# Joint attention block with 64-wide values tiles and re-placed transfers, and new orders in turned rows, route, second layer and last products of an attention-MoE kernel

## The chip, the cores and the metric

The kernel runs on one core of a Trainium2 chip. The metric is device time of one execution in microseconds; several runs are summed up by their median. The engines are TensorE (PE, with its weight loads as PEld), VectorE (DVE), ScalarE (ACT), GpSimd (POOL) and SyncE (SP), which issues most of the DMAs.

## The reference

Three parts follow one another: attention with a bias that a small MLP makes from positions, a top-1 mixture of experts with a capacity, and a two-matrix layer with h·cos(h).

```python
scores = scale * np.matmul(q, k.transpose(0, 1, 3, 2))        # B 2, H 8, S 576, D 64
h = np.maximum((psi_rel / psi_i)[..., None] @ w1 + b1, 0.0)   # log1p tables, hidden 32
scores = scores + (h @ w2).transpose(2, 0, 1)[None]
attn = np.exp(scores - np.max(scores, axis=-1, keepdims=True))
attn = attn / (np.sum(attn, axis=-1, keepdims=True) + 1e-09)
x = np.matmul(attn, v)                                        # to 1152 rows of 512
...
expert_idx = np.argmax(x @ w_gate, axis=1)                    # 8 experts
# the first 288 rows of each expert, in order, are kept
h = np.maximum(np.einsum('ecd,edf->ecf', disp, w1), 0.0)
y = np.einsum('ecf,efd->ecd', h, w2)
out[i] = gate_w[i] * y[expert_idx[i], pos[i]]                 # kept rows only
...
h = x @ w_in                                                  # 512 -> 2048
g = h * np.cos(h)
return g @ w_out
```

## The kernel before, in words

**Attention** (some 24 to 176 us) goes through 36 steps. A step is a batch, a block of 128 query rows and a pair of heads p; a block is four steps. `BLOCKS` orders them: (batch, block) (0,0), (1,0), (0,1), (1,1), then the **joint block** (block 4, which has only 64 rows, of both batches at once; steps 16 to 19), then (0,2), (1,2), (0,3), (1,3). `step_of(n)` writes a step out by hand: q·k products of step n+1 (`emit_qk`), the sum of scores and bias with the row minimum on DVE (`emit_sum`), the exponential on ACT (`emit_exp`), the transposes of step n (`emit_tr`) and their copies to SBUF on ACT (`emit_tev`), the values products of step n-1 (`emit_pv`) and their eviction (`emit_xs`), and the bias of group n+10 (`bias_h`, `bias_half`). At a step's end SP issues that step's transfers. Each engine runs its instructions in the order in which they are written here; `manual_schedule` reorders nothing. With the trace, the start of a step is the first q·k product (L403) that it issues.

**Bias.** 40 groups of rows: h = relu of a table row on DVE or ACT (L319 is on ACT, L321 on DVE; four quads to a group), a product (L347), the eviction with a scale into a row buffer `ev` (L351, L353), and a transfer from there to its place (L328, for the joint block L338). From group 14 on three `ev` buffers are used in rotation. The joint block's bias lands for one batch's 64 partitions; `double(p)` (L835) copies it on SP for the other batch, two heads at a time, in four steps from `DOUBLE_AT`. `fill_rows` (L840) and `fill_out` (L843) write zeros to the dispatch rows and to the output, at `FILL_AT` and `OUT_AT`. `emit_pv` makes the values products in column tiles of 32, four of them side by side; in the joint block separately for each batch, over 64 streamed columns instead of 128.

**Mixture of experts.** `route()` takes logits, the expert, the gate (L586 to L593) and the place of each row through running counts `srun`. The two fullest experts and a small one are done in straight line, others under a branch that isn't taken here. The fullest is chosen early, the second choice (L684 to L677) at `SECOND_CHOICE`. Expert 0's rows are gathered, turned by PE (`turned`, L990) and split into high and low parts (`xh` L991, `xl` L992), because a 32-bit product is made of three products of such parts. Its first products (L1018) start in the last attention steps. `e0_mid` and `e0_side` are tables of what goes between them; `f1` in them is the logits product of the last block (L544).

**Second layer** (some 246 to 352 us) has 16 slices f of 128 hidden columns. `first(f)` gives h on PE (L1281), in two parts of columns; `gate(f)` makes g of it: turns (copies on ACT, L1388, L1389), turn (L1392, DVE), sine (L1395, ACT), product (L1399, DVE), high (gh, L1402, ACT), low_ (gl, L1405, DVE). `second(f)` adds the slice's products into five tiles of 128 rows of output (L1377). The weights w_in and w_out are 64-bit numbers; `narrow` makes 32-bit ones of a piece by bit operations: mag (ACT, L754), then shift, low and sign (DVE, L757, L760, L763). `splitwi` and `splitwo` split them (high parts L962 on ACT, low parts L964 on DVE). `between(f)` sets the order of gate, narrowing and splits. At the end ACT and DVE evict the five tiles (L1362, L1364) and POOL stores them by indirect DMA (L1365).

## Time and profile before

| what | value |
|---|---|
| median of 3 runs | 361.13 us (360.67 to 361.41) |
| profiled execution | 361.79 us, its span 360.0 us |
[...]
| PE busy | 341.8 us, 95% of the span |
| DVE busy | 293.9 us, 82% |
| ACT busy | 266.8 us, 74% |
| POOL busy | 37.7 us, 10% |
| instruction queues | 37 packets (0.61 MB) and 24 packets (0.20 MB) |

The time is 1.8 us longer than the span, which goes from the first to the last instruction. An engine's busy share is an average over phases with different limits. In the timeline a line gives the start, the busy time, the engine, the line of the kernel, the operation, its output and input, the number of like operations in a row, and in brackets the idle time before it with what ended it. Matmul records overlap: the distance of two starts is what one costs, not its busy time.

### The profile page before, as it was taken

The numbers are of one execution on the slowest core, as the hardware profiler recorded it, in microseconds if no ns is written. First come the engines' busy times: TensorE is split into PE (matmuls) and PEld (weight loads), VectorE is DVE, ScalarE is ACT, GpSimd is POOL, SyncE is SP. The second block draws the span as 40 slices with busy tenths as digits, with TensorE's granted clock in tenths as the row PEclk, the third lists the DMA queues.
The fourth block names the chain that finished last, engine by engine and source line by source line (L and its number), as shares of the span: only waits on it lengthen the run. The fifth ranks groups of instructions, "written<-read, shape, count | busy, mean of one in ns | idle before, by whom it ended". The sixth has DMA issues, their size and how long they took to land. (4 is left out here: it accounts for less than half of the span.)

```text
span 360.0 us, 11244 instructions
## 1 busy us (share of the span) xinstructions
PE 341.8 (95%) x4459; PEld 272.8 (76%) x4459; DVE 293.9 (82%) x771; ACT 266.8 (74%) x627; POOL 37.7 (10%) x89
## 2 busy tenths in 40 slices
PE   7989999999989999898999999999999999999991
PEld 6346777775656777686789999968898898898880
DVE  5988889898869886988799999887997887876760
ACT  6768999987978898898943597387777667666560
POOL 3000001101001420110007112100000000000023
PEclk9999999999999999999999999999999999999997
DMA  7799966679976687799238698943243242110003
GB/s 234 203 246 278 251 168 194 203 157 258 277 244 190 205 247 192 249 258 310 90 109 309 167 353 280 295 157 119 66 121 107 91 131 73 58 62 0 2 28 117
DMA packets 47023, 63.89 MB, mean 177 GB/s; under 512 B 5772, under 2 KB 30476, under 8 KB 46962
## 3 DMA queue, kind: packets, MB, share of 16 engines
q1 hardware_dynamic: 45666, 60.24, 57.8%
q0 software_dynamic: 1152, 2.48, 1.9%
q8 instruction: 37, 0.61, 0.7%
q10 hardware_dynamic: 144, 0.36, 0.3%
q14 instruction: 24, 0.20, 0.2%
HBM read 41.08 MB, written 11.47 MB: 146 GB/s over the span
## 5 line engine op out<-in xcount | busy, mean ns | idle before, releaser
L420 ACT ACTIVATE e<-e,mn 128x576 f32<-128x576 f32 x72 | 56.2, 781 | 14.8 <-DVE mn L411 14.8
L321 DVE TENSOR_SCALAR h<-tt,sml 128x576 f32<-128x576 f32 x122 | 57.0, 513 | 0.1
L451 ACT ACTIVATE et<-t 128x512 f32<-128x512 f32 x72 | 38.7, 593 | 0.0
L347 PE MATMUL bb<-h,sml 128*32 128x288 f32 x400 | 35.6, 412 | 1.1 <-DVE h L321 0.6
L428 PEld LDWEIGHTS t<-ident,e 64*128 64x128 f32 x576 | 24.3, 139 | 8.9 <-issue 1.8
L403 PE MATMUL sb<-k,q 64*128 64x288 f32 (+1 forms) x160 | 27.0, 449 | 0.4 <-DVE lp L556 0.3
L353 ACT ACTIVATE wo<-bb,sml 128x288 f32<-128x288 f32 x49 | 24.7, 504 | 3.5 <-PE bb L347 2.1
L428 PE MATMUL t<-ident,e 64*128 64x64 f32 x576 | 26.1, 225 | 1.1 <-ACT e L420 0.8
L1281 PE MATMUL t<-yh,s1h 128*128 128x352 f32 (+1 forms) x88 | 26.8, 305 | 0.0
L1281 PE MATMUL t<-yh,s1l 128*128 128x352 f32 (+1 forms) x88 | 26.6, 303 | 0.0
L1281 PE MATMUL t<-yl,s1h 128*128 128x352 f32 (+1 forms) x88 | 26.5, 302 | 0.0
L1392 DVE TENSOR_TENSOR tn<-tn,kn 128x608 f32<-128x608 f32 (+2 forms) x18 | 13.0, 722 | 15.8 <-ACT kn L1389 15.7
L470 PE MATMUL sa<-et,wi 128*32 128x128 f32 (+1 forms) x800 | 23.0, 260 | 1.6 <-issue 1.6
L1402 ACT ACTIVATE gh<-tn 128x608 fp32r<-128x608 f32 (+2 forms) x18 | 11.8, 656 | 17.0 <-DVE tn L1399 17.0
L403 PE MATMUL sa<-k,q 64*128 64x288 f32 (+1 forms) x160 | 23.8, 406 | 0.0
L470 PEld LDWEIGHTS sa<-et,wi 128*32 128x32 f32 x800 | 19.5, 110 | 3.9 <-issue 1.7
L403 PEld LDWEIGHTS sb<-k,q 64*128 64x128 f32 (+1 forms) x160 | 10.5, 174 | 14.7 <-issue 6.0
L1018 PE MATMUL hp<-xh,s1h 128*128 128x288 f32 x64 | 19.5, 305 | 0.0
L1377 PE MATMUL hp<-s2h,gh 128*128 128x512 f32 x48 | 19.1, 399 | 0.0
L1021 ACT ACTIVATE hh<-hp 128x288 fp32r<-128x288 f32 x16 | 6.5, 409 | 17.0 <-PE hp L1018 17.0
L1377 PE MATMUL hp<-s2l,gh 128*128 128x512 f32 x48 | 19.0, 396 | 0.0
L1377 PE MATMUL hp<-s2h,gl 128*128 128x512 f32 x48 | 18.9, 394 | 0.0
(308 smaller groups left out, 999.9 us busy)
## 6 DMA issues: line engine op xcount, KB each, us to landing
keep<-win SPq DMA_DIRECT2D x16, 512.0 KB
keep<-wout SPq DMA_DIRECT2D x16, 512.0 KB
w1r<-mw SPq DMA_DIRECT2D x12, 512.0 KB
w2r<-mw SPq DMA_DIRECT2D x12, 512.0 KB
disp<-wo SPq DMA_DIRECT2D x10, 516.0 KB
bias<-wo SPq DMA_DIRECT2D x15, 288.0 KB
q<-qd SPq DMA_DIRECT2D x8, 512.0 KB
k<-kd SPq DMA_DIRECT2D x8, 288.0 KB
```

What stands on the lines that cost most here:

```text
L321: V.tensor_scalar(out=h, in0=win_, scalar1=col, scalar2=0.0, op0=ALU.add, op1=ALU.max)
L347: T.matmul(out=ps[32 * j:32 * j + 32, :], lhsT=w2s, rhs=h_t[g, j][:, cols], start=True, stop=True)
L353: A.activation(out=ev_t[g][:, cols], in_=ps, func=AF.Copy, scale=rst[:, g:g + 1])
L403: T.matmul(out=ps[a:e, half, 0:HS], lhsT=qt[b, ib][rows_, h, a:e], rhs=kt[c, p][rows_, u, :], start=True, stop=True)
L420: A.activation(out=e_t[n][:, u], in_=e_t[n][:, u], func=AF.Exp, scale=-1.0, bias=mn_t[n][:, u:u + 1], accum_out=z_t[b, ib][:, h:h + 1],)
L428: T.transpose(ps, src[half], ident[half, half])
L451: A.activation(out=et_t[n][:, 0:8, 64 * g:64 * g + 64], in_=halves[g], func=AF.Copy)
L470: T.matmul(out=xo[32 * i:32 * i + 32], lhsT=v_of(c, p, at_, 32), rhs=et[:, 4 if j == 4 else 5 * u + j, a:e], start=(j == 4), stop=(j == 3),)
L1018: T.matmul(out=ps, lhsT=a[g % 3][:, k], rhs=x[:, k], start=(k == 0 and i == 0), stop=(k == 3 and i == 2))
L1281: done.append(T.matmul(out=sums(f, i), lhsT=w[f % 3][:, k], rhs=ya[k][x][:, o0 + a:o0 + e], start=(k == 0 and n == 0), stop=(k == 3 and n ...
L1377: T.matmul(out=oacc[t][rows_of(t)], lhsT=x, rhs=b[f % 3], start=(f == 0 and n == 0), stop=(f == 15 and n == 2))
L1392: V.tensor_tensor(out=tn, in0=tn, in1=kn, op=ALU.subtract)
```

## The change

Eight places change.

1. `emit_pv` uses column tiles of 64 for the joint block (20 calls a step instead of 40; the trace shows each as two records).
2. Groups 14 to 26 have five `ev` buffers in rotation instead of three, and on SP `FILL_AT` has 10 for 13, `DOUBLE_AT` goes from 10 to 12, and the first three `OUT_AT` from 10, 12, 12 to 8, 9, 11.
3. `SECOND_CHOICE` goes from 27 to 26, with the load that follows it.
4. In `route()` the counts `srun` come behind the products `jk` and `pv` when they are on DVE.
5. Quads 0 (on ACT) and 1 (on DVE) of group 10's h are made ahead of the first sums instead of in step 0.
6. `turned(0)` makes rows 0 and 1 in the hook "turned" of step 34 instead of "values", in other banks, and copies their high parts on DVE instead of ACT.
7. `f1` goes from place 2 to place 1 of `e0_mid`.
8. In the second layer, f=1 and f=14 have an order of their own, the splits of f=0 move into f=1, tiles 3 and 4 of `second(13)` move behind `first(15)`, and the last products have a new order.

SP's queue around the doublings, before (SP; `wi<-wi` are the doublings, `wi<-wo` the joint bias rows, `keep<-wo` other bias rows, `out_dram<-wo` and `disp<-wo` the zero rows):

```order
L840 DMA disp<-wo 256x1x516
L338 DMA wi<-wo 8x8x576 x2
L835 DMA wi<-wi 64x2x576
L843 DMA out_dram<-wo 128x512
L328 DMA keep<-wo 16x8x576
L306 DMA q_91<-qd 128x8x64 x2
L835 DMA wi<-wi 64x2x576
L328 DMA keep<-wo 16x8x576
```

and now:

```order
L340 DMA wi<-wo 8x8x576 x2
L848 DMA disp<-wo 256x1x516
L330 DMA keep<-wo 16x8x576
L308 DMA q_91<-qd 128x8x64 x2
L851 DMA out_dram<-wo 128x512
L330 DMA keep<-wo 16x8x576
L843 DMA wi<-wi 64x2x576
L330 DMA keep<-wo 16x8x576
L843 DMA wi<-wi 64x2x576
```

The first doubling stood right behind the last joint rows; now two other bias rows, the loads of q and a fill stand between them.

DVE around the second choice in steps 27 and 28, before (DVE; `e,mn<-sb,bias` and `e,mn<-sa,bias` are the two sums of a step, `cnt`, `top`, `ix`, `some` and `hot` the second choice):

```order
L411 ISA e,mn<-sb,bias_156 128x576
L411 ISA mn 128x1
L411 ISA e,mn<-sa,bias_156 128x576
...
L631 SCALAR_TENSOR_TENSOR sl<-idxf,ov 128x1
L684 SCALAR_TENSOR_TENSOR cnt<-gone,cnt 128x8
L674 MAX top_74<-cnt 128x8
L675 MAX_INDEX ix_81<-top_74,cnt 128x8
L676 CAST some<-ix_81 128x1
L677 TENSOR_SCALAR hot<-eio,some 128x8
L489 TENSOR_SCALAR rz<-z 128x4
```

and now:

```order
L510 TENSOR_TENSOR wo<-xb,rz 128x128
L692 SCALAR_TENSOR_TENSOR cnt<-gone,cnt 128x8
L682 MAX top_74<-cnt 128x8
L683 MAX_INDEX ix_81<-top_74,cnt 128x8
L684 CAST some<-ix_81 128x1
L685 TENSOR_SCALAR hot<-eio,some 128x8
L413 ISA e,mn<-sb,bias_156 128x576
L413 ISA mn 128x1
L413 ISA e,mn<-sa,bias_156 128x576
```

The five operations stood behind these two sums and ahead of the next step's; now they stand ahead of these two.

DVE at f=14, before (DVE; L757, L760 and L763 are shift, low and sign of the last narrowing):

```order
L1392 TENSOR_TENSOR tn_4126<-tn_4126,kn_4127 128x608
L757 TENSOR_SCALAR wo<-wo 128x512
L760 SCALAR_TENSOR_TENSOR wo<-keep,wo 128x512
L1399 TENSOR_TENSOR tn_4126<-t_138,tn_4126 128x352
L1399 TENSOR_TENSOR tn_4126<-bb,tn_4126 128x256
L763 SCALAR_TENSOR_TENSOR wo<-keep,wo 128x512
L1405 TENSOR_TENSOR gl_4134<-tn_4126,gh_4131 128x608
L964 TENSOR_TENSOR s2l_117<-wo,s2h_114 128x512
```

and now, DVE first, then ACT at the same place (s2h is the high part of the narrowed weight, the L1400 behind it the gate's first copy of f=15):

```order
L1404 TENSOR_TENSOR tn_4046<-tn_4046,kn_4047 128x608
L1411 TENSOR_TENSOR tn_4046<-t_138,tn_4046 128x352
L1411 TENSOR_TENSOR tn_4046<-bb,tn_4046 128x256
L765 TENSOR_SCALAR wo<-wo 128x512
L768 SCALAR_TENSOR_TENSOR wo<-keep,wo 128x512
L1417 TENSOR_TENSOR gl_4054<-tn_4046,gh_4051 128x608
L771 SCALAR_TENSOR_TENSOR wo<-keep,wo 128x512
L973 TENSOR_TENSOR s2l_117<-wo,s2h_114 128x512
```

```order
L1401 ACTIVATE kn_4047<-tn_4046 128x608
L1407 ACTIVATE tn_4046<-tn_4046 128x608
L762 ACTIVATE wo<-keep 128x512
L1414 ACTIVATE gh_4051<-tn_4046 128x608
L971 ACTIVATE s2h_114<-wo 128x512
L1400 ACTIVATE tn_4044<-t_137 128x352
```

Shift and low moved behind the product and sign behind gl; on ACT the mag moved behind the sine, and s2h still stands ahead of the gate of f=15.

The diff:

```diff
@@ -39,10 +39,10 @@
 MAGS = 28, 29, 30, 31, 33
 LOWS = {28: 3, 29: 2, 30: 2, 31: 3, 32: 2, 35: 3}
 ROUTE_FROM = 17
-FILL_AT = 6, 7, 8, 9, 13, 14, 15, 16, 17, 18, 19
-DOUBLE_AT = 10
-OUT_AT = 10, 12, 12, 20, 20, 21, 21, 22, 22
-SECOND_CHOICE = 27
+FILL_AT = 6, 7, 8, 9, 10, 14, 15, 16, 17, 18, 19
+DOUBLE_AT = 12
+OUT_AT = 8, 9, 11, 20, 20, 21, 21, 22, 22
+SECOND_CHOICE = 26
 PLAIN = 26
 LATE_FROM = 32
 LATE_A = {33: 1}
@@ -185,7 +185,9 @@
     base = 9 * RW + 2 * NP * 128
     lt_buf = cut(base, 128)
     ev_buf = [cut(base + 144 + S * i, S) for i in range(3)]
-    ev_first = dict(zip(range(8, 14), ev_buf + [cut(a, S) for a in (6 * RW + 60, S * 3, S * 2)]))
+    ev_more = [cut(S * i, S) for i in (3, 2)]
+    ev_at = dict(zip(range(8, 14), ev_buf + [cut(6 * RW + 60, S)] + ev_more))
+    ev_at.update({g: (ev_buf + ev_more)[(g - 14) % 5] for g in range(14, 27)})
     v13 = cut(base + 144 + 3 * S, 640)
 
 
@@ -341,7 +343,7 @@
 
     def bias_half(g, half, bank=bb):
         if half == 0:
-            ev_t[g] = ev_first.get(g, ev_buf[g % 3])
+            ev_t[g] = ev_at.get(g, ev_buf[g % 3])
         cols, ps = slice(half * 288, half * 288 + 288), bank[:, :288]
         for j in range(4):
             T.matmul(out=ps[32 * j:32 * j + 32, :], lhsT=w2s, rhs=h_t[g, j][:, cols], start=True, stop=True)
@@ -361,7 +363,7 @@
     lead_t = {}
 
     def bias_lead(g):
-        ev_t[g] = bias_a[:, g] if g < 8 else ev_first[g]
+        ev_t[g] = bias_a[:, g] if g < 8 else ev_at[g]
         lead_t[g] = (xb, bb) if g == 9 else (t0, t1) if g % 3 == 2 else [s_bank[1 - g % 3][:, i] for i in range(2)]
         for half in range(2):
             for j in range(4):
@@ -460,15 +462,15 @@
 
     def emit_pv(n):
         b, ib, p = steps[n]
-        et = et_t[n]
-        et_t.pop(n)
+        et = et_t.pop(n)
+        w = 64 if b == BOTH else 32
         for c, a, e in [(c, 64 * c, 64 * c + 64) for c in range(B)] if b == BOTH else [(b, 0, 128)]:
             xo = sum_of(n)[:, a:e]
             for j in (4, 0, 1, 2, 3):
-                for i in range(4):
-                    u, at_ = i // 2, 512 + 32 * i if j == 4 else 64 * (4 * (i // 2) + j) + 32 * (i % 2)
+                for i in range(128 // w):
+                    u, at_ = w * i // 64, 512 + w * i if j == 4 else 64 * (4 * (w * i // 64) + j) + w * i % 64
                     T.matmul(
-                        out=xo[32 * i:32 * i + 32], lhsT=v_of(c, p, at_, 32),
+                        out=xo[w * i:w * i + w], lhsT=v_of(c, p, at_, w),
                         rhs=et[:, 4 if j == 4 else 5 * u + j, a:e], start=(j == 4), stop=(j == 3),
                     )
         if p == 0:
@@ -609,8 +611,12 @@
                     T.matmul(out=psr[:, E * i:E * i + E], lhsT=w, rhs=x, start=(j == 0), stop=(j == len(before)))
             yield
             made_up()
-            for t in ts:
-                aux[0].tensor_tensor(out=srun, in0=srun, in1=oh[:, t, :], op=ALU.add)
+            def count():
+                for t in ts:
+                    aux[0].tensor_tensor(out=srun, in0=srun, in1=oh[:, t, :], op=ALU.add)
+
+            if aux[0] is P:
+                count()
             eng = V if len(ts) > 1 and aux[0] is V else P
 
             k, at_ = len(ts), slice(ts[0], ts[-1] + 1)
@@ -620,6 +626,8 @@
             jk = sm_p.tile([128, 5, E], F32, tag="jk", bufs=1, name="jk")[:, 0:k]
             V.tensor_tensor(out=jk, in0=psr[:, 0:E * k].rearrange("p (t e) -> p t e", e=E), in1=oh[:, at_, :], op=ALU.mult)
             V.tensor_reduce(out=pv, in_=jk, axis=AX.X, op=ALU.add)
+            if aux[0] is V:
+                count()
             eng.tensor_scalar(out=ov, in0=pv, scalar1=float(CAP), scalar2=float(NOROW), op0=ALU.is_ge, op1=ALU.mult)
             eng.tensor_tensor(out=ov, in0=ov, in1=pv, op=ALU.add)
             if ts[0] >= 3:
@@ -853,6 +861,7 @@
             fetch_k(1, 0)
     load_v(0, (2,))
     fetch_k(1, 1)
+    bias_h(LEAD, on_act=(0,), quads=(0, 1))
     warm(8)
     emit_sum(0, 0)
     emit_sum(0, 1)
@@ -891,7 +900,7 @@
             if p == 0 and 0 < j < len(BLOCKS) - 1:
                 fetch_q(*BLOCKS[j + 1])
             if n == 0:
-                bias_h(g)
+                bias_h(g, quads=(2, 3))
             emit_exp(n + 1, 0)
         if n == ns - 4:
             aux[0] = V
@@ -985,10 +994,13 @@
     def turned(s, ks=range(4)):
 
         for k in ks:
-            ps = hp[(8 * s + k) % 3] if k < 3 else acc[3] if s == 0 else xb[:, 0:CAP]
+            ps = (hp[2], acc[3], hp[0], hp[2])[k] if s == 0 else hp[(8 + k) % 3] if k < 3 else xb[:, 0:CAP]
             for c in range(3):
                 T.transpose(ps[:, 96 * c:96 * c + 96], xg[:, c, 128 * k:128 * k + 128], ident[:96, :96])
-            A.activation(out=xh[:, k], in_=ps, func=AF.Copy)
+            if s == 0 and k < 2:
+                V.tensor_copy(xh[:, k], ps)
+            else:
+                A.activation(out=xh[:, k], in_=ps, func=AF.Copy)
             V.tensor_tensor(out=xl[:, k], in0=ps, in1=xh[:, k].bitcast(F32), op=ALU.subtract)
 
     def second(s, m):
@@ -1060,8 +1072,8 @@
         (32, "values"): [lambda: split1(0, V, "l")],
         (33, "end"): [lambda: fetch_w2(eid[0], (2,))],
         (34, "first"): [lambda: split1(1, V, "h")],
-        (34, "turned"): [part_banks],
-        (34, "values"): [lambda: turned(0, (0, 1)), lambda: split1(1, V, "l")],
+        (34, "turned"): [part_banks, lambda: turned(0, (0, 1))],
+        (34, "values"): [lambda: split1(1, V, "l")],
         (34, "end"): [lambda: fetch_w2(eid[0], (3,))],
         (35, "start"): [lambda: turned(0, (2, 3))],
         (35, "values"): [lambda: split2(0), lambda: next(e0)],
@@ -1232,7 +1244,7 @@
         (1, [last_pair]), (2, [f2, f3, f4]), (3, [last_route, second_expert]), (4, [make_list]), (5, [pick_few]), (7, [count_rest]),
     ):
         e0_side[m][0:0] = fs
-    e0_mid.update({1: [lambda: ids_of(0)], 2: [f1], 6: [lambda: ids_on(0, 128, slice(0, CAP))]})
+    e0_mid.update({1: [f1, lambda: ids_of(0)], 6: [lambda: ids_on(0, 128, slice(0, CAP))]})
     for m, (a, c) in enumerate((((0,), (0,)), ((1,), ()), ((), (1,)), ((2,), ()), ((), (2,)), ((3,), (3,)))):
         e0_side[m] += [lambda a=a: fetch_w1(eid[1], a), lambda c=c: fetch_w2(eid[1], c)]
     e0_side[6].append(fetch_third)
@@ -1413,7 +1425,11 @@
             take = lambda what: [what.pop(0)] if what else []
             if 0 < f < 15:
                 turns, turn, sine, product, high, low_ = gate(f, 0, WM)
-                order = [turns, *take(mags), turn, *take(lows), sine, *take(lows), *mags, product, high, *take(lows), low_, *lows]
+                if f in (1, 14):
+                    parts = [lambda: splitwi(3, V), lambda: splitwo(1, V)] if f == 1 else []
+                    order = [turns, turn, *parts, sine, product, *mags, *take(lows), high, *take(lows), low_, *lows]
+                else:
+                    order = [turns, *take(mags), turn, *take(lows), sine, *take(lows), *mags, product, high, *take(lows), low_, *lows]
             else:
                 both = [gate(f, *p) for i, p in enumerate(parts_) if i not in gated]
                 order = [s for steps_ in zip(*both) for s in steps_]
@@ -1421,25 +1437,24 @@
                     order = [both[i][j] for i, j in ((0, 0), (0, 1), (0, 2), (1, 0), (0, 3), (0, 4), (1, 1), (0, 5), (1, 2), (1, 3), (1, 4), (1, 5))]
             for s in order:
                 s()
-            if f < 13:
+            if 0 < f < 13:
                 splitwi(f + 3, V)
-            if f < 15:
+            if 0 < f < 15:
                 splitwo(f + 1, V)
 
         begun, gated = few(gate) if few else ({}, ())
         for f in range(16):
             first(f, o0, [i for i in (0, 1) if i not in begun.get(f, ())])
-            if 0 < f < 15:
-                second(f - 1)
-            elif f > 0:
-                second(14, (0, 1, 2))
+            if f > 0:
+                second(f - 1, range(NT) if f < 14 else (0, 1, 2))
             between(f, gated if f == 0 else ())
 
 
+        second(13, (3,))
         second(15, (0, 1, 2))
         for t in (3, 4):
-            second(14, (t,))
-            second(15, (t,))
+            for f in range(13 if t > 3 else 14, 16):
+                second(f, (t,))
 
     second_layer(0, range(SECOND_TO, NPC), lambda gate: expert_few(range(MID, SECOND_TO), gate))
     yst.close()
```

## Rows read from the trace of the kernel before

**Rows 1.** Timeline of ACT at the start: start us, busy us, engine, line, operation.

```profile
23.17 0.78 ACT L420 ACTIVATE e<-e,mn 128x576 f32<-128x576 f32 x1 [1.21 <-DVE mn L411]
...
27.93 0.50 ACT L353 ACTIVATE wo<-bb,sml 128x288 f32<-128x288 f32 x1 [2.10 <-PE bb L347]
```

**Rows 2.** Timeline of DVE in the same stretch.

```profile
25.36 3.52 DVE L321 TENSOR_SCALAR h<-tt,sml 128x576 f32<-128x576 f32 x8
```

**Rows 3.** Timeline of PE, first products of steps 6, 7, 14 and 15.

```profile
49.55 0.76 PE L403 MATMUL sb<-k,q 64*128 64x288 f32 x4
...
54.04 0.76 PE L403 MATMUL sb<-k,q 64*128 64x288 f32 x4
...
83.71 0.76 PE L403 MATMUL sb<-k,q 64*128 64x288 f32 x4
...
88.96 0.71 PE L403 MATMUL sb<-k,q 64*64 64x288 f32 x8
```

**Rows 4.** Timeline of ACT in step 14.

```profile
87.78 0.50 ACT L353 ACTIVATE wo<-bb,sml 128x288 f32<-128x288 f32 x1 [1.37 <-DMA keep<-wo]
```

**Rows 5.** Timeline of SP's queue, 66 to 92 us.

```profile
79.61 0.60 SPq L328 DMA_DIRECT2D keep<-wo  x1
80.26 1.45 SPq L835 DMA_DIRECT2D wi<-wi  x1
```

**Rows 6.** Waits of SP's queue, 40 to 90 us: total us, times, longest.

```profile
SPq L835 <- DMA wi<-wo: 4.2, 1, 4.2
```

**Rows 7.** Timeline of PE, values products in steps 17, 20 and 21.

```profile
102.82 0.54 PE L470 MATMUL sa<-et,wi 128*32 128x64 f32 x24 [1.56 <-issue]
...
116.90 0.59 PE L470 MATMUL sa<-et,wo 128*32 128x64 f32 x27 [0.50 <-issue]
...
120.62 1.30 PE L470 MATMUL sa<-et,wi 128*32 128x128 f32 x40
```

**Rows 8.** DMA queues, 98 to 104 us: packets, MB, share of 16 engines.

```profile
q8 instruction: 1, 0.02, 1.2%
```

**Rows 9.** Timeline of DVE in steps 27 and 28.

```profile
143.71 0.76 DVE L411 CUSTOM_DVE_ANT_0 e<-sb,bias 128x576 f32<-128x576 f32 x1 [0.73 <-PE sb L403]
...
146.93 0.16 DVE L684 SCALAR_TENSOR_TENSOR cnt<-gone,cnt 128x8 f32<-128x8 f32 x1
```

**Rows 10.** Timeline of ACT in step 28.

```profile
149.06 0.78 ACT L420 ACTIVATE e<-e,mn 128x576 f32<-128x576 f32 x1 [0.99 <-DVE mn L411]
```

**Rows 11.** Timeline of DVE in step 34.

```profile
174.96 0.15 DVE L586 TENSOR_SCALAR gates<-es 128x1 f32<-128x1 f32 x1 [1.73 <-ACT ex L580]
```

**Rows 12.** Timeline of ACT in step 34.

```profile
174.81 0.72 ACT L991 ACTIVATE xh<-hp 128x288 fp32r<-128x288 f32 x2
```

**Rows 13.** Timeline of PE at f1 in loop 1, and at f=1.

```profile
187.53 0.43 PE L544 MATMUL xb<-wo,wgs 128*32 128x128 f32 x8 [0.38 <-DVE jk L621]
...
253.84 0.39 PE L1281 MATMUL bb<-yh,s1h 128*128 128x256 f32 x1 [0.43 <-DVE tn L1399]
```

**Rows 14.** Timeline of DVE at f=14.

```profile
339.90 0.42 DVE L757 TENSOR_SCALAR wo<-wo 128x512 int32<-128x512 int32 x1
340.36 0.69 DVE L760 SCALAR_TENSOR_TENSOR wo<-keep,wo 128x512 int32<-128x512 int32 x1
340.97 0.52 DVE L1399 TENSOR_TENSOR tn<-t,tn 128x352 f32<-128x352 f32 x1
...
341.73 0.68 DVE L763 SCALAR_TENSOR_TENSOR wo<-keep,wo 128x512 int32<-128x512 int32 x1
342.65 0.79 DVE L1405 TENSOR_TENSOR gl<-tn,gh 128x608 fp32r<-128x608 f32 x1 [0.24 <-ACT gh L1402]
```

**Rows 15.** Timeline of ACT at the end of f=14.

```profile
342.53 0.61 ACT L962 ACTIVATE s2h<-wo 128x512 fp32r<-128x512 f32 x1
343.45 0.46 ACT L1388 ACTIVATE tn<-t 128x352 f32<-128x352 f32 x1 [0.31 <-PE t L1281]
```

**Rows 16.** Timeline of POOL at the end.

```profile
348.84 0.99 POOL L1365 DMA_INDIRECT out_dram<-o,idt  x1 [119.49 <-ACT o L1364]
```

## The prediction

> **What bounds the kernel now.** I read the busy table of the page first, then the timeline of TensorE (PE) step by step, looking for places where it is idle or where a step is longer than its twin, then the timelines of ACT, DVE, POOL and SP at just those places, and last the queues. PE is busy for nearly the whole span (the small table above), so a gap on PE is worth its full length if what follows on PE has its data. The exception is the end, where the stores on POOL run on after PE has finished. What a measurement can tell from no change is about 0.2%, 0.72 us here. The profiled execution took 361.79 us, 0.66 above the median of 361.13; the sum is made against the first, and the median moved by the same amount.
>
> **The start (group 10's h).** ACT stands idle for 1.21 us before the first exponential, and that ACT pass over 128x576 takes 0.78 [rows 1], so the h of the same size that ACT now makes there is free. DVE makes eight h after its first sums, 3.52 us or 0.44 each [rows 2], and ACT's next eviction waits 2.10 us for the product over them [rows 1]. Two of the eight go: 0.88 less on that path. One of them now stands on DVE ahead of the first sums and delays them by 0.44. The net gain is 0.44; bounds 0.2 (part of it was covered) and 0.55. I take **-0.4**.
>
> **Transfers ahead of the joint block.** Two steps that stand at the same place in their blocks take, from the first q-k product of one to that of the next, 54.04 - 49.55 = 4.49 us and 88.96 - 83.71 = 5.25 us [rows 3]. In the second, ACT waits 1.37 us for a transfer out of the row buffer that it wants to write [rows 4]. SP issued that transfer at 79.61 [rows 5], 8.2 us before ACT could write at 87.78. SP was late with it because the first doubling waits 4.2 us there for the joint bias rows to land [rows 6], and all that is queued behind waits too. Now the doublings stand two steps later, and five buffers instead of three give two more steps until one is written again. The step falls back to its twin: 0.76; bounds 0.3 (another wait ends just ahead of this one) and 1.37. I take **-0.75**. The out-stores and the fill that move on SP are wanted much later, and POOL's queue is as it was. The price is that the first doubling comes later: the old kernel issued the doubling of that step (its third) at 80.26 [rows 5]; with 8.2 us to land and the 0.4 from the start, the first one is there by 88.1. The joint sum that reads it stands behind the products at 88.96, 0.71 long [rows 3]: wanted at 89.67, now 1.15 earlier, at 88.5. That leaves 0.4 us, more if SP gets there sooner without its stop. I cost it at nothing.
>
> **Wide values tiles in the joint block.** In two of the four joint steps PE stops inside the values product and waits for nothing that the profile shows ("issue"): 1.56 and 0.50 us, together 2.06 [rows 7]. Such a step issues 80 products of 64 streamed columns into 32-wide tiles, four side by side; 24 of them take 0.54 us when nothing stops them, while a step outside the block issues 40 products of 128 columns in 1.30 us without a stop [rows 7]. The streaming time is about the same; the joint step asks for twice the instructions in it. In the 6 us around the first stop the instruction queue moved one packet of 0.02 MB [rows 8], so I take the stops for instructions that come too slowly. The change halves them: 40 in a step, two side by side. The nearest rows for pairs: eight products of 64*64 take 0.71 us where four of 64*128 take 0.76 [rows 3], so 64-wide pairs do overlap, and the stream costs what it did. The stops go: **-2.05**, since the same rate outside the block shows none; bounds 0 and 2.06.
>
> [...]
>
> **Second choice.** Five small DVE operations, the first at 146.93, stand before a sum for which ACT's exponential waits 0.99 us [rows 9, 10]. They take about 1.0 us. In their new place they stand before a sum ahead of which DVE is idle for 0.73 us, waiting for PE [rows 9], so about 0.3 of them shows there, and up to 0.99 goes here. Their load on SP comes one step sooner, past transfers that nobody waits for. **-0.65**; bounds 0.3 and 0.9.
>
> **Turned rows of expert 0.** DVE is idle for 1.73 us before the gates of a route step, waiting for ACT [rows 11]. The two casts of turned rows, 0.72 us on ACT [rows 12], go there, with the transposes and the two differences that stood behind them. ACT comes to the last exponential sooner, and PE behind it. Part of the 0.72 was covered by the transposes that PE had ahead: **-0.5**; bounds 0.2 and 0.8.
>
> **Logits of the last block, one group earlier.** PE waits 0.38 us for the route that stands beside them [rows 13]. In the new place they have to wait for the last eviction of values instead. I take **-0.1**; bounds -0.38 and +0.3. The route's counts that now stand behind its products make its chain about 1 us shorter, but PE waits for it nowhere else: nothing.
>
> **Second layer, f=1.** PE waits 0.43 us for the gate's product on DVE [rows 13], which a shift and a low of a narrowing held up. These, and the splits that move here from f=0, now stand behind turn or product. The wait goes: **-0.45**; bounds 0.2 and 0.7 (the pause of the pipeline around the wait included).
>
> **f=14 and the last products.** Second products of f=13 move behind the last first products, which then come earlier. But the gate of f=15 begins with an ACT copy, which stands in ACT's order behind s2h of the last narrowed weight, and s2h reads what the sign wrote. Before, shift starts at 339.90, low at 340.36, product at 340.97, sign at 341.73 and gl at 342.65 [rows 14], s2h at 342.53 and the gate's copy at 343.45, after 0.31 us of waiting for PE [rows 15]. In the new order the product waits for the sine alone: I put it at 340.75, an ACT pass of some 0.75 after the turn that ends at 339.90. It takes 0.76 (340.97 to 341.73), to 341.5; then shift 0.46 and low 0.61 (the distances in rows 14) and gl 0.72 (0.79 less overlap): sign starts at 343.3 and ends at 344.0. The copy s2h starts there, and the gate's copy 0.55 later at 344.55 instead of 343.45. PE, sooner done with its first products, waits for the gate; POOL's first store, at 348.84 behind the last eviction's copy [rows 16], follows the gate, and the four behind it follow each other. **+1.1**; bounds -0.3 (the copy's wait for PE goes and nothing else holds it) and +1.35 (another 0.24, the idle in gl's row).
>
> **Sum.** -0.4 - 0.75 - 2.05 - 0.65 - 0.5 - 0.1 - 0.45 + 1.1 = -3.8. The profiled 361.79 becomes 358.0, the median 361.13 becomes **357.3 us**.
>
> **Rivals.**
> 1. *The stops stay* or move to another place in the instruction stream: 357.3 + 2.05 = 359.4. For: only two of four joint steps have one, and they differ in size, so the number of products alone doesn't set them. Against: 40 products in a step pass without one [rows 7]. [...] Chance 0.22.
> 2. *The end gains.* If something in the new order brings sign ahead of s2h's turn, the gate's copy starts 0.31 sooner instead of 1.1 later: 357.3 - 1.4 = 355.9. Against: the engines run in order. Chance 0.14.
> 3. *Pairs don't run side by side.* Each joint values product, about 1.1 us, takes twice that, in four steps: the stops go, 4.4 comes: 361.7, no change. Against: [rows 3]. Chance 0.06.
> 4. *The doublings land too late*, slower than before. Place: the first joint sum. It decides from a landing of 8.2 + 0.4 = 8.6 us on; then DVE waits, PE behind it, one us for one us. At 8.6 + 3.8 = 12.4 us all gains are gone, and from 13.1 the kernel is slower by over 0.2%; at 14 it gives 357.3 + 5.4 = 362.7. For: the only landing that I go by is one row transfer's. Against: SP no longer stops in front of it. Chance 0.06; a landing one or two us late lies in the range.
> 5. *Half of the small gains are lost downstream* (start, transfers, second choice, turned rows), since another engine holds the same step: 357.3 + 1.15 = 358.5. Chance 0.1.
>
> **Numbers.** My forecast has the remaining 0.42. The range takes in rivals 1, 2 and 5 with some width: 355.7 to 359.8. Outside lie rivals 3 and 4 and the outer edges of 1 and 2, not quite 0.2 together. Faster by over 0.2% (below 360.4): 0.42 + 0.22 + 0.14 + 0.1 = 0.88; within 0.2%: rival 3, 0.06; slower: rival 4, 0.06.
>
> **What the next profile would show.** Right: joint values products without "issue" idle, at about 1.1 us each; the first step before the block near 4.5 us, and no eviction waiting for a transfer; no small DVE operations before the sum near 147; no PE wait at f=1; at f=14 sign behind gl, the gate's copy behind s2h, and PE waiting before the second products of f=15. Wrong: a stop of PE in a joint step, a joint sum that waits for DMA, values products of 2 us, or a gate of f=15 that starts before 343.

## The result and the profile after

| | before | changed |
|---|---|---|
| median (6 runs each, same chip) | 361.41 us (360.67 to 363.47) | 358.68 us (357.95 to 360.71) |
| ratio, 95% interval | | 0.9899 (0.9866 to 0.9933) |
| profiled execution, span | 361.79, 360.0 us | 360.71, 359.0 us |

The medians differ by 2.73 us; 3.8 had been forecast, and 357.3 us for the time. The ratio is an estimate of its own from the runs and not the quotient of these two medians (0.9924); it puts the gain at 3.65 us, 2.4 to 4.8. The profiled execution of the changed kernel is the slowest of its six, by 1.2 us, and this matters below: its own time isn't the kernel's usual one.

The first view is the timeline of PE, the first product of steps 5, 6, 14 and 15, to be read against [rows 3]:

```profile
45.02 0.76 PE L405 MATMUL sb<-k,q 64*128 64x288 f32 x4
...
51.12 0.76 PE L405 MATMUL sb<-k,q 64*128 64x288 f32 x4
...
85.88 0.76 PE L405 MATMUL sb<-k,q 64*128 64x288 f32 x4
90.36 0.71 PE L405 MATMUL sb<-k,q 64*64 64x288 f32 x8
```

Step 14 takes 90.36 - 85.88 = 4.48 us where it took 5.25; its twin took 4.49. Step 5 takes 51.12 - 45.02 = 6.10, where it took 4.31 before (45.24 to 49.55), though nothing in it was changed. The same timeline shows most of the reason, in two places:

```profile
46.10 0.28 PE L430 MATMUL t<-ident,e 64*128 64x64 f32 x3
47.99 0.65 PE L430 MATMUL t<-ident,e 64*128 64x64 f32 x13 [1.61 <-issue]
...
54.72 1.08 PE L472 MATMUL sa<-et,v 128*32 128x128 f32 x32 [0.40 <-issue]
```

These are stops like those of [rows 7], with nothing to wait for, but in steps 5 and 6, and one of them in the transposes. In the joint steps there is none (timeline of PE, the values products made in steps 17 and 18, 64-wide now; those of steps 19 and 20 are like the last two rows):

```profile
101.36 1.39 PE L472 MATMUL sa<-et,wi 128*64 128x64 f32 x40
...
106.07 0.80 PE L472 MATMUL sa<-et,wi 128*64 128x64 f32 x20
106.71 0.75 PE L472 MATMUL sa<-et,v 128*64 128x64 f32 x20
```

At the start ACT waits less for the product over h, and DVE makes six h behind the sums instead of eight (ACT, then DVE; [rows 1, 2]):

```profile
23.81 0.78 ACT L422 ACTIVATE e<-e,mn 128x576 f32<-128x576 f32 x1 [0.98 <-DVE mn L413]
...
27.70 0.50 ACT L355 ACTIVATE wo<-bb,sml 128x288 f32<-128x288 f32 x1 [1.24 <-PE bb L349]
```

```profile
25.99 2.66 DVE L323 TENSOR_SCALAR h<-tt,sml 128x576 f32<-128x576 f32 x6
```

The first exponential starts at 23.81 instead of 23.17, the eviction at 27.70 instead of 27.93. The second choice stands ahead of the sum of step 27 now, and ACT's exponential of step 28 (147.76) waits for nothing (DVE, then ACT; [rows 9, 10]):

```profile
142.22 0.16 DVE L692 SCALAR_TENSOR_TENSOR cnt<-gone,cnt 128x8 f32<-128x8 f32 x1
...
143.42 0.76 DVE L413 CUSTOM_DVE_ANT_0 e<-sb,bias 128x576 f32<-128x576 f32 x1
```

```profile
147.76 0.78 ACT L422 ACTIVATE e<-e,mn 128x576 f32<-128x576 f32 x1
```

At f=14 and f=15, DVE, ACT, PE and POOL in turn ([rows 14 to 16]):

```profile
336.73 0.79 DVE L1404 TENSOR_TENSOR tn<-tn,kn 128x608 f32<-128x608 f32 x1 [2.03 <-ACT kn L1401]
...
338.30 0.53 DVE L1411 TENSOR_TENSOR tn<-t,tn 128x352 f32<-128x352 f32 x1 [0.78 <-ACT tn L1407]
338.74 0.41 DVE L1411 TENSOR_TENSOR tn<-bb,tn 128x256 f32<-128x256 f32 x1
339.07 0.42 DVE L765 TENSOR_SCALAR wo<-wo 128x512 int32<-128x512 int32 x1
339.52 0.69 DVE L768 SCALAR_TENSOR_TENSOR wo<-keep,wo 128x512 int32<-128x512 int32 x1
340.13 0.78 DVE L1417 TENSOR_TENSOR gl<-tn,gh 128x608 fp32r<-128x608 f32 x1
340.83 0.69 DVE L771 SCALAR_TENSOR_TENSOR wo<-keep,wo 128x512 int32<-128x512 int32 x1
```

```profile
341.55 0.63 ACT L971 ACTIVATE s2h<-wo 128x512 fp32r<-128x512 f32 x1 [1.59 <-DVE wo L771]
342.09 0.45 ACT L1400 ACTIVATE tn<-t 128x352 f32<-128x352 f32 x1
```

```profile
345.31 0.50 PE L1389 MATMUL xb<-s2h,gh 128*128 128x512 f32 x1 [1.51 <-ACT gh L1414]
```

```profile
347.46 0.99 POOL L1377 DMA_INDIRECT out_dram<-o,idt  x1 [119.87 <-ACT o L1376]
```

ACT idles 1.59 us for the sign, the gate's first copy waits behind s2h, PE waits 1.51 us. Counted from DVE's turn at f=14, the gate's first copy comes 342.09 - 336.73 = 5.36 us later; before it came 343.45 - 339.19 = 4.26 us later, with this row for the turn (DVE before; the copy is in [rows 15]):

```profile
339.19 0.79 DVE L1392 TENSOR_TENSOR tn<-tn,kn 128x608 f32<-128x608 f32 x1 [2.03 <-ACT kn L1389]
```

Here the change costs time.

Where the 1.0 us between the two spans went, by the time at which the same instruction starts (changed minus before, running difference):

| up to | running | this part |
|---|---|---|
| second step | -0.22 | start -0.22 |
| step 8 | +2.18 | stops in steps 5 and 6, +2.40 |
| step 15 | +1.40 | transfers -0.77 (step 14) |
| step 17 | +0.95 | steps 15 and 16, -0.45 |
| step 21 | -0.68 | joint values products -1.63 |
| step 29 | -1.26 | second choice: +0.26 in step 27, -0.84 in step 28 |
| first product of expert 0 | -1.55 | turned rows -0.29 |
| behind the last block's logits | -1.74 | -0.19 |
| behind f=1 | -2.47 | -0.73 |
| first store on POOL | -1.38 | last products and f=14, +1.09 |
| end of the span | -1.0 | +0.4 behind the stores |

### The profile page after: what moved, and what is told of

Read it like the earlier page. It is cut to its first block, busy times and chain, and to the rows that moved or that the text cites. A ratio compares the mean times of both kernels' runs of the same rounds, so it can differ in the third digit from the quotient of the medians.

```text
span 359.0 us, 10922 instructions
## 1 busy us (share of the span) xinstructions
PE 341.6 (95%) x4299; PEld 273.3 (76%) x4299; DVE 294.1 (82%) x772; ACT 266.9 (74%) x626; POOL 37.4 (10%) x89
## 5 line engine op out<-in xcount | busy, mean ns | idle before, releaser
L472 PEld LDWEIGHTS sa<-et,wi 128*32 128x32 f32 (+1 forms) x700 | 19.7, 114 | 2.4 <-DVE mn L413 1.5
L1030 PE MATMUL hp<-xh,s1l 128*128 128x288 f32 x64 | 18.9, 296 | 0.0
```

The lines of the kernel that those rows point to most:

```text
L472: T.matmul(out=xo[w * i:w * i + w], lhsT=v_of(c, p, at_, w), rhs=et[:, 4 if j == 4 else 5 * u + j, a:e], start=(j == 4), stop=(j == 3),)
L1030: T.matmul(out=ps, lhsT=a[g % 3][:, k], rhs=x[:, k], start=(k == 0 and i == 0), stop=(k == 3 and i == 2))
```

## The experiments

Four sets of runs, on three chips (the third and fourth on the same one); the kernel before ran in each set and its median was 362.57, 364.01, 363.35 and 363.48 us there. So medians are compared within a set, or by their ratio to before. Of an edit, the code shows only the lines from which the others follow.

**First set: are the stops those of the place, or of late instructions?**

The changed kernel again, no edit.

> The changed kernel again, to see a second profiled execution. Theory A (late instruction packets: the stops are PE running out of instructions because a 16 KB packet waited behind bulk transfers): the stop of 1.6 us in step 5 depends on that execution; here it is smaller or gone, any stop lies 1.5 to 2 us behind the end of an instruction packet, and none lies in the joint block. Time 358 to 359.5. Theory B (the stop belongs to the program at that place): the same 1.6 us at the same transposes in step 5.

Measured 358.48 us (8 runs, 357.99 to 359.91), ratio 0.9909 (0.9875 to 0.9942). Its profiled execution (357.99, span 356.3) has no stop anywhere; step 5 takes 4.31 us. So the sizes 1.61 and 0.40 us belong to one execution. The place belongs to the program all the same: at the instruction of the 1.61 us PE stops in three other profiles of the experiments below, for 0.39, 0.50 and 0.52 us, and in ten not at all.

The kernel before with wide tiles alone:

```diff
-                for i in range(4):
+                for i in range(128 // w):        # w = 64 if b == BOTH else 32
```

> The kernel before with 64-wide values tiles in the joint block and nothing else. Theory A: no issue stop in the joint steps, values product of a joint step still about 1.1 us, time 1 to 2 us below before (0.9945 to 0.997). Theory B (the stop only moves): the same total of 2 us of stops elsewhere, time as before within 0.5 us.

Measured 361.76 us (12 runs), ratio 0.9970 (0.9941 to 0.9999), 0.8 us below before. The interval only just leaves out 1. No stop in a joint values product, but one of the old size just ahead of them: in step 16, in the values product that belongs to step 15, the last before the block (timeline of PE):

```profile
98.41 0.52 PE L470 MATMUL sa<-et,wo 128*32 128x128 f32 x10 [1.53 <-issue]
```

The changed kernel with `w = 32`:

> The changed kernel with 32-wide values tiles in the joint block again. Theory A: issue stops of 0.5 to 2 us in the joint steps come back, time 1 to 2 us above the changed kernel. Theory B: no difference beyond 0.5 us.

Measured 359.51 us (10 runs), ratio 0.9920 (0.9891 to 0.9950), 1.0 above the changed kernel in the same set, with ratio intervals that overlap. The stop is back at the instruction where it was before, after 56 of the 80 products of step 17, and so is the one of step 20 (117.39, 0.22 us); and the narrow product without a stop starts at 107.32, with the next instruction at 108.46, 1.14 us later:

```profile
100.97 0.96 PE L472 MATMUL sa<-et,wi 128*32 128x64 f32 x56
103.58 0.54 PE L472 MATMUL sa<-et,wi 128*32 128x64 f32 x24 [1.66 <-issue]
...
107.32 0.77 PE L472 MATMUL sa<-et,wi 128*32 128x64 f32 x40
107.90 0.74 PE L472 MATMUL sa<-et,v 128*32 128x64 f32 x40
108.46 0.67 PE L349 MATMUL bb<-h,sml 128*32 128x288 f32 x8
```

In the run of the changed kernel above, the wide product of the same place takes 103.97 to 105.28, 1.31 us:

```profile
103.97 0.80 PE L472 MATMUL sa<-et,wi 128*64 128x64 f32 x20
104.60 0.75 PE L472 MATMUL sa<-et,v 128*64 128x64 f32 x20
105.28 0.69 PE L349 MATMUL bb<-h,sml 128*32 128x288 f32 x8
```

64-wide tiles in every step (`w = 64`):

> The changed kernel with 64-wide values tiles in every step: 40 instructions (20 products and 20 weight loads) fewer in each of 32 steps more. Theory A: PE asks for instructions more slowly, so there are no stops in the startup steps either; time 0 to 1.5 us below the changed kernel; a values product stays about 1.1 us. If pairs of 64-wide tiles don't overlap at 128 columns, a values product takes 2 us and the kernel loses 30 us. Theory B: nothing but noise.

Measured 363.35 us (12 runs, 363.09 to 364.27), 4.9 above the changed kernel. No stop at all, the steadiest of all runs, but a values product outside the block takes 48.99 to 50.24, 1.25 us, instead of 1.10 (94.82 to 95.92 in the run of the changed kernel), 0.15 more in 32 steps:

```profile
48.99 1.31 PE L472 MATMUL sa<-et,wi 128*64 128x128 f32 x20
50.24 0.69 PE L349 MATMUL bb<-h,sml 128*32 128x288 f32 x8
```

Two things follow. Halving the instructions takes the stops out of the joint values products: in all ten profiles with 64-wide joint tiles, those of the later sets included, none of these products has one, and in all three with 32-wide tiles (before, this one and the one of the fourth set) both stops are there, at the same two instructions. It doesn't rid the kernel of them, as 98.41 above and steps 5 and 6 show, so what it is worth as a time is what the medians say, 0.8 and 1.0 us, near the edge of the noise. And wide tiles have a price of their own, 0.17 us in a joint step, that my sum put at nothing.

**Second set: the old order at f=14, and the start and transfers taken apart.**

```diff
-                if f in (1, 14):
+                if f == 1:
```

> The changed kernel with the old order at f=14 (narrowing ahead of the product, sign ahead of gl); f=1 and the last products stay as changed. Theory A (the gate of f=15 is held by s2h, which waits for sign): s2h comes right behind gh, the gate's first copy 1.4 to 1.5 us earlier against the DVE turn of f=14, PE's wait of 1.51 us before the second products of f=15 goes, the first store on POOL comes 1.4 us earlier, time 1.2 to 1.5 us below the changed kernel (0.996). Rival B (the new order pays because gl is ready sooner for the second products of f=14): PE waits for gl there instead, time the same or up to 1 us longer.

Measured 357.20 us (6 runs, 355.99 to 357.69), ratio 0.9847 (0.9803 to 0.9891), the fastest of all; 1.2 below the fastest other kernel of the set, whose runs (357.80 to 359.42) don't overlap with these. The changed kernel itself didn't run in this set. DVE's turn, then ACT, PE and POOL:

```profile
334.06 0.79 DVE L1404 TENSOR_TENSOR tn<-tn,kn 128x608 f32<-128x608 f32 x1 [2.03 <-ACT kn L1401]
```

```profile
337.39 0.61 ACT L971 ACTIVATE s2h<-wo 128x512 fp32r<-128x512 f32 x1
337.91 0.45 ACT L1400 ACTIVATE tn<-t 128x352 f32<-128x352 f32 x1
```

```profile
341.14 0.50 PE L1389 MATMUL xb<-s2h,gh 128*128 128x512 f32 x1
```

```profile
343.29 0.99 POOL L1377 DMA_INDIRECT out_dram<-o,idt  x1 [118.30 <-ACT o L1376]
```

The idle of 1.59 us on ACT and the 1.51 us on PE are gone. DVE's turn at f=14 starts at 334.06 here and at 336.73 in the changed kernel; from there the gate's first copy comes 3.85 us later instead of 5.36, and the first store 9.23 instead of 10.73, 1.50 less. PE waits nowhere for gl. Rival B falls.

The start as before (without the early `bias_h`):

> The changed kernel without the two early h of group 10 at the start. Theory A: the first step's first product comes 0.4 to 0.6 us earlier, the second step 0.2 us later than in the changed kernel; time 0.2 us longer, not to be told from no change. Rival B (the early DVE pass delays the sums by more than it saves): 0.2 to 0.5 us shorter.

Measured 359.16 us (8 runs), ratio 0.9898 (0.9861 to 0.9935). The first step starts at 23.25 and the second at 28.36, against 23.61 and 27.86 in the kernel with the old order at f=14: the second step comes 0.5 us later, more than the 0.22 of the changed kernel's profile; as a time it is within the scatter of the medians.

Three row buffers again, `ev_at` with `ev_buf[g % 3]`:

> The changed kernel with three row buffers in rotation instead of five, SP's new places kept. Theory A (it is the queue held by the doubling that made the row transfer late, the buffers only add slack): no eviction waits for a transfer for over 0.3 us, time as the changed kernel within 0.3 us. Rival B (the buffers are what matters): a wait of 0.5 us or more on keep<-wo near step 14 and 0.5 to 1 us longer.

The old places on SP with five buffers (`DOUBLE_AT = 10` and the two old lists):

> The changed kernel with the old places of fill, doubling and out-stores on SP, five row buffers kept. Theory A: the doubling again waits some 4 us on SP; with five buffers that costs nothing at step 14, time within 0.3 us of the changed kernel. Rival B (SP's hold delays another wait, a load or the next row): 0.5 to 1 us longer with a wait for DMA on ACT or DVE in steps 10 to 16.

Measured 358.36 us (6 runs; 0.9881, 0.9837 to 0.9925) and 359.89 us (12 runs, 357.59 to 362.33; 0.9915, 0.9881 to 0.9949). In both profiles step 14 takes 4.49 us and no eviction waits for a transfer, though in the second SP still stands at the doublings (waits of SP's queue: total, times, longest):

```profile
SPq L843 <- DMA wi<-wo: 5.4, 2, 4.9
```

Either half of this part takes the wait of step 14 away alone; they don't add. The 1.5 us between the two medians isn't explained by step 14. In the second one's profile PE stops once, 0.38 us in step 16, in the first one's once, 0.39 us in step 5, and the second one's runs scatter most (357.59 to 362.33); I leave the cause open.

**Third set: what is left, and more traffic.**

Both early h on ACT, with the old order at f=14 (`on_act=(0, 1)`):

> The changed kernel with the old order at f=14 and both early h of group 10 on ACT instead of one on ACT and one on DVE. Theory A: ACT is free for both (it waited about 1 us before the first exponential), so the first sums on DVE come 0.44 us earlier; the first step starts 0.2 to 0.45 us earlier; time 0.2 to 0.4 us below the version with the old order at f=14 alone, 356.5 to 357.2. Rival B: the second h on ACT ends later than the first sum and delays the exponential; no gain.

Measured 358.97 us (6 runs, 358.09 to 361.90), ratio 0.9884 (0.9838 to 0.9931). The steps start at 23.30 and 27.55, 0.56 earlier than in the last kernel of this set (23.86, 28.11), a little more than expected; but the median is not better. Its profiled execution has stops of 0.52 us in step 5 and of 1.30 in step 32, more than the gain; whether the other executions have them isn't known. As a time the test is inconclusive.

More transfers, in the version with the old order at f=14:

```diff
+        if 15 <= n < 20:
+            for j in (0, 1, 2):
+                fill_out(j)
```

> The version with the old order at f=14 with more bulk transfers: in steps 15 to 19 SP issues three of the 256 KB zero stores to the output again, 3.9 MB more in all; nothing that is computed changes. Theory A (packets of instructions wait behind bulk transfers): stops of PE with nothing to wait for come back in steps 15 to 20 although the values tiles are 64 wide, together 1 us or more, each right behind a late packet, besides waits for data. Theory B (only PE's own rate of instructions matters): no stop; waits for transfers on ACT and DVE alone.

Measured 364.24 us (10 runs), ratio 1.0026 (0.9994 to 1.0057). My Theory A asked for stops and there is none: instead one sum waits for bias rows, with PE behind it for 4.62 us (DVE, then PE):

```profile
111.18 0.76 DVE L413 CUSTOM_DVE_ANT_0 e<-sb,keep 128x576 f32<-128x576 f32 x1 [5.06 <-DMA keep<-wo]
```

```profile
112.00 0.37 PE L430 MATMUL sb<-ident,e 64*128 64x64 f32 x2 [4.62 <-DVE mn L413]
```

PE stood still for 4.62 us in just these steps, and whether instructions caught up in that time isn't shown, so this run doesn't tell the theories apart. It does show what late rows cost, and that is more than the wait: behind these 4.62 us without work PE's products took longer, eight records of the bias product 1.12 us (112.41 to 113.53) where eight took 0.62 in step 18 (102.83 to 103.45), and the joint values product 2.33 us (113.78 to 116.11) where that of step 18 took 1.32 (103.71 to 105.03). PE's mean granted clock in this execution is 0.986 of full speed, against 0.993 and 0.995 in the other two profiles of the set. Step 19 took 117.23 - 105.65 = 11.58 us instead of 4.69 in the run of the changed kernel above.

64-wide tiles in two joint steps, `w = 64 if n in (16, 17) else 32`, with the old order at f=14:

> The version with the old order at f=14 with 64-wide tiles in the first two joint steps alone, 32-wide ones in the other two. The wide product costs 1.31 us where the narrow one took 1.14, so two narrow steps save 0.34 us. Theory A: the third and fourth joint steps stand close to a stop with narrow tiles; in some executions 0.5 us of it comes, so the time is within 0.4 us of the version with the old order at f=14. Theory B: 0.3 us less.

Measured 358.44 us (6 runs), ratio 0.9852 (0.9816 to 0.9888), not to be told from 0.9847. The two narrow steps are 0.2 us shorter each and have no stop in this execution.

**Fourth set: less traffic at the stop.** The narrow kernel, with six fills left out, those of steps 14 to 19: `FILL_AT = 6, 7, 8, 9, 10` and nothing behind.

> The changed kernel with 32-wide values tiles in the joint block (as the run that brought the stop back), but without the last six zero fills of the dispatch rows, 516 KB each but the last, in steps 14 to 19. It leaves these fills out, so rows of experts that are never filled hold what was there. Theory A (instruction packets wait behind bulk transfers): with less traffic in front of them the packets come sooner after they are due, and the stops of 0.5 to 1.7 us in the joint steps go though the tiles are narrow; time 0.5 to 1.5 us below the narrow kernel with its fills. Theory B (the joint step's own rate of instructions is enough): a stop of 0.5 us or more stays in the joint steps, time as with the fills.

Measured 360.81 us (12 runs), ratio 0.9917 (0.9885 to 0.9948), as the narrow kernel with its fills (0.9920): the 0.5 to 1.5 us that Theory A wanted are not there. The place itself says more. The stop comes after the same 56 products, and lasts 0.24 us where it lasted 1.66; a second, of 0.43 us, stays in step 20, where it lasted 0.22. (This profile also has 0.50 us in step 5, where no fill was left out, and 0.29 at 196.42.)

```profile
100.49 0.96 PE L472 MATMUL sa<-et,wi 128*32 128x64 f32 x56
101.69 0.54 PE L472 MATMUL sa<-et,wi 128*32 128x64 f32 x24 [0.24 <-issue]
...
115.72 0.49 PE L472 MATMUL sa<-et,wo 128*32 128x64 f32 x21 [0.43 <-issue]
```

The queues in the window ahead of the stop in which its packet of instructions starts, with the fills (100.4 to 101.9 us) and then without them (98.7 to 100.1 us); columns are packets, MB, share of 16 engines:

```profile
q1 hardware_dynamic: 227, 0.45, 95.7%
q8 instruction: 1, 0.02, 5.5%
```

```profile
q1 hardware_dynamic: 27, 0.04, 13.7%
q8 instruction: 1, 0.02, 5.8%
```

By the trace's record of each packet, it ended 3.79 us after the start of step 17 with the fills (102.13, step from 98.34) and 2.51 us without them (100.38, step from 97.87): 1.28 earlier, and the stop is 1.42 shorter. The packet itself took as long, 1.31 and 1.30 us; it started later. So traffic sets most of the size of the large stop, by one execution of each kernel. The stop of step 20 didn't shrink, and in step 5 the transfers that the program asks for don't decide alone: from 39.6 to 45.5 us, ahead of the stop of 1.61 us, the changed kernel's first profile gives the bulk queue q1 a share of 107.6% of the 16 engines, and the same program has no stop there in its second. Each theory was half right, and what sets the size in steps 5 and 20 stays open.

**All stops together.** In the profiles of all these kernels PE has twelve stops by "issue" of over 0.3 us, and the one of 0.24. Each ends 1.3 to 1.7 us behind the end of the latest 16 KB packet of the instruction queue q8: 102.82 behind 101.54 and 116.90 behind 115.21 before, 47.99 behind 46.51 and 54.72 behind 53.40 in the changed kernel, 103.58 behind 102.13 in the narrow one, 162.44 behind 160.94 in the third set. Counting PE's recorded instructions, products and weight loads, from the start of the trace, the two stops before stand 767 apart, and the two after 255, so three times and once some 256. The packets of q8 come about as often: 33 for 8338 recorded instructions of PE before (28.16 to 340.84 us) and 31 for 7830 in the changed kernel's first profile (28.19 to 321.51 us), one for 253 in both. I call a stretch of 256 such instructions a block. That one packet brings one block is my estimate from these counts; what a packet holds isn't shown.

The same count settles what the distances alone leave open. All thirteen stops stand at one of six instructions, number 1218, 1473, 3266, 3522, 4289 or 5826, and each of these is a multiple of 256 plus 193 or 194. So they always stand at the same distance into a block, as they must if PE stops where a packet's instructions begin (the count leaves out what the trace doesn't record, so the distance itself needn't be 0). The 0.29 at 196.42 stands elsewhere, at 7013, with no packet just ahead of it; it is something else. In the narrow joint steps the 256 instructions of a block last 4.4 us without a stop (107.26 to 111.70 before), in the wide ones 7.2 (101.50 to 108.66 in the changed kernel's second profile), which by the same estimate leaves the next packet more time. At the large stop the block ahead of it began at 97.32 with the fills and at 96.84 without; the packet ended 4.81 and 3.54 us later, and without its stop PE would have been through after 4.60 and 4.61.

## Why the prediction was right, and where not

The time lies in the range, on its slow side of the middle. Against the forecast 3.8 the medians give 2.73, a good quarter less; the ratio gives 3.65, with an interval of 2.4 to 4.8 that holds the forecast. In the profile the spans differ by 1.0; without the 2.40 of steps 5 and 6 it would be 3.4. That this lies near 3.8 is in part luck: the wide tiles, the start and the turned rows gave less than their terms, f=1 gave more, and steps 15 and 16 gave 0.45 that stood in no term. Point by point:

- *The start*, -0.4: -0.22 in the profile, 0.5 by the experiment's second step. Right in kind. The half that I put on DVE ahead of the sums is a choice of the change that costs 0.5 us at the first step (23.86 against 23.30 with both h on ACT).
- *Transfers*, -0.75: -0.77, from the twin step. The mechanism was named as two causes that work together; in the profiles of the experiments either remedy alone is enough. The doublings were not late, as costed: no joint sum waits for a transfer. Steps 15 and 16 gave 0.45 more that I hadn't seen; some 0.2 of it is a small stop in step 16 before (38 records of its values product took 1.51 us, where 40 take 1.28 after).
- *Wide tiles*, -2.05: this is the term that was mis-sized, in two ways. "The stream costs what it did" was wrong: 1.31 us instead of 1.14, 0.68 in four steps. I had read [rows 3], eight 64*64 products against four of 64*128, as the price of pairs, and that row has other weights and longer streams. And the 2.06 us were one execution's: the two stops last 1.88 and 0.67 together in the other two narrow profiles, the narrow kernel loses 1.0 us against the wide one by their medians, and 0.8 is what wide tiles alone gain. The direction was right, and the cause that the argument named, instructions that come too slowly, fits the runs: with the packet 1.28 us earlier the large stop was 1.42 us shorter. That PE stops in steps outside the block stood in no term; my first rival had the stops move, and in the profiled execution 2.0 us of them stood in steps 5 and 6, about what it is slower than the median.
- *Second choice*, -0.65: -0.58. The cost ahead, 0.27, was 0.26.
- *Turned rows*, -0.5: -0.29. The casts went to DVE's idle time, the gates behind them start at 174.23, and the next copy on ACT (175.65) waits 0.48 us for PE; so more of the 0.72 was covered than I took.
- *Logits*, -0.1: -0.19; the new wait is the predicted one, PE waits 0.40 us for the eviction of values.
- *f=1*, -0.45: -0.73, just over my bound of 0.7: the wait of 0.43 is gone, and another 0.3 with it, which I had only put into the bound.
- *f=14 and the last products*, +1.1: +1.09, PE's wait 1.51. The chain sign, s2h, gate was read from the order alone and holds to the digit: 344.55 - 339.19 = 5.36 us from the turn to the gate's copy were forecast, and 5.36 measured. My sign of being wrong, a gate of f=15 before 343, came by the clock alone (342.09), since the turn itself comes 2.46 us earlier than before; it should have been counted from the turn. The second set showed the cause: with the old order there, 1.50 us less up to the first store, and a median 1.2 below the next kernel. My second rival, that the end gains, is what that kernel does (3.85 us from the turn, against 4.26 before).

The second choice, the turned rows, the logits and f=1 were tested by no run of their own: these numbers are read from one execution.

The rivals with pairs that don't overlap and with late doublings did not come. The version with all changes but the order at f=14 beats the kernel before, 0.9847 (0.9803 to 0.9891); that it beats the changed one (0.9899, 0.9866 to 0.9933) the profiles show better than these intervals, which overlap.

## What to carry to other kernels

A stop that names no releaser is a size of one execution (1.61 us in one profile of the changed kernel, none in the next): look at it in a second profile before it goes into a sum, and look for the instruction packet in front of it. When instructions are moved on one in-order engine, follow what stands behind them on the next in-order engine too: the order at f=14 took two operations from in front of a product on DVE and held ACT for 1.59 us. And a row that is near in shape isn't a price; two halves of a change can remove the same wait, so their gains don't add.

## What the runs showed of the hardware that I had not expected

In straight-line code PE stopped where nothing that the profile shows held it: 0.24 to 1.66 us, at the same instructions in different executions, all at the same distance into a stretch of 256 of its recorded instructions, and 1.3 to 1.7 us behind the end of a 16 KB packet. At one place the size went with the bulk transfers (1.66 us with 95.7% share of their queue, 0.24 with 13.7%). Column tiles of 64 in pairs take 1.31 us for what tiles of 32 in fours do in 1.14. And behind a wait of 4.62 us on PE eight records of the bias product took 1.12 us, where eight had taken 0.62 before it.
